# A scan over tokens with eight routed experts: one-bank PSUM tiles for the experts, alternating output banks, and small steps of the scan on GpSimd

## The chip, the core and the metric

One core of a Trainium2 chip runs the whole kernel. The metric is device time in microseconds, from the first instruction to the last. Three runs of the kernel before give a median of 426.35 us (425.26 to 426.58).

Names: PE is TensorE (PEld its weight loads), DVE VectorE, ACT ScalarE, POOL or GpSimd the fourth compute engine, SP the engine that issues most loads. PSUM, in which PE puts its products, has eight banks of 2 KB for each of 128 partitions; the other engines copy or add out of it into SBUF.

## What is computed

A state-space scan over 4 batches x 8 heads x 768 tokens (head size 32, state size 16), then a router that sends each of the 3072 tokens to one of eight experts, by cosine against the experts' embeddings:

```python
for c in range(nc):                      # chunks along the sequence
    cum = cumsum(log_a of the chunk); L = exp(cum_i - cum_j), i >= j
    M = (C @ B^T) * L
    y = M @ x + (C @ state) * exp(cum)
    state = exp(sum(log_a)) * state + sum_j B_j x_j * exp(cum_last - cum_j)
x = y as (3072, 256)
logits = (x/|x|) @ (emb/|emb|).T / tau
e = argmax(logits); gate = probs[e]
out[token] = gate * (relu(x @ w1[e]) @ w2[e])      # 256 -> 1024 -> 256
```

## The kernel before, in words

**Start and scan** (begin(), 1153; scan(), 1188). The sequence is cut into 6 chunks of 128 tokens; a step handles one chunk of two of the four batches, so there are 12 steps. For each step load() (272) brings c, b and x on SP's queue two chunks ahead; scale_c() (285) and scale_x() (306) multiply them by decays and their inverses, on GpSimd except in chunk 0; split_c() (297) masks into two halves on ACT. On PE, inner() (320, L328) multiplies C by B into pg, causal() (335, L338) masks that on DVE, outputs() (344, L354 with the state, L365 within the chunk) goes into py, sums() (372, L379) makes the new part of the state in py, and states() (386) with pass_on() (413) adds it to the old state and scales it, on DVE: reads of PSUM at L399 to L404 and the scaled state at L416. keep_outputs() (422) copies to SBUF on ACT, finish() (430, L434) turns the result to token order and appends the logits in pz, keep_tokens() (440) copies it and keep_rows() (448) writes a chunk's rows to DRAM on SP's queue.

The decays of all heads are computed by decays() (155, last operation L169) for chunks 0 to 3 at the start and for 4 and 5 after step 1. keep_decays() (182, L186) permutes them on PE, writes them to DRAM (fd), and spread_decays() (192) reads them back, repeated over state rows, into F with four DMAs a chunk. For chunk 0, spread_first() (202) does it on PE. scale_emb() (246, L252 to L255) and turn_emb() (258) prepare the router's embeddings; route_consts() (99) makes constants on GpSimd.

Routing goes chunk by chunk behind the scan: pick() (455, last operation L467) makes one-hots of the best expert, count() (472) adds them up, ranks() (479, L487) counts on PE how many tokens of the same expert come before, hots() (492) makes of that a place in a table of 104-row tiles, tables() (527, L530) and add_table() (535) put token numbers there.

**Experts** (moe(), 1317). early() (1309) starts a first job J0 with the first 208 tokens of expert 0 from chunks 0 to 3, while the scan ends; a second job J1 holds further tokens of expert 0, then come seven jobs of up to 416 tokens. gather() (683, L687) fetches a job's tokens by four indirect loads on GpSimd, squares() (694) and gates1() to gates3() make the gate, turn() and keep_turned() (730, 737) transpose the input. J0 uses plain products (plain_up(), 871; plain_down(), 882, L887). All the others use a scheme of seven block products in place of eight: up() (760, L763) for each of two groups g and p = 1 to 7, down() (819, L823) for p = 1 to 7. A product goes into one of three banks of a set (760: `BANK = {1: 0, 6: 0, 7: 0, 4: 0, 2: 1, 5: 2, 3: 2}`), further products are added there, and keep() (771, L775, ACT), c11() to c22() (783 to 797, DVE L785, L789, L793) or o11() to o22() (828 to 842, L831, L835) read the bank between them. turn_out() (846, L850) transposes an output of 104 tokens into the fourth bank, send() (854) scales it by the gate on ACT (L857) and writes it with an indirect DMA on GpSimd (L860). weight_sums() (646) makes the sums of weight blocks that the scheme needs.

**Order.** Everything runs under a manual schedule: each engine works in the order of the code. work_on() (894) writes out one round: the up blocks of job J mixed with the outputs of the job before and the transposes of the next, then the down blocks, mixed with the weights' sums and the first two up blocks of the next job (begin_job(), 961). leftover() (966) counts at the end whether tokens are left that fit in no job, and branches (L998).

**PSUM.** Lines 1376 to 1381 allot the eight banks as three tiles, and take the experts' banks as slices of them:

```python
k.pg = ps.tile([128, 4, 512], F32, name="pg")
k.py = ps.tile([128, 2, 512], F32, name="py")
k.pz = ps.tile([128, 2, 512], F32, name="pz")
k.sets = [[k.pg[:, i] for i in range(3)], [k.py[:, 0], k.py[:, 1], k.pz[:, 0]]]
k.tb = [k.pg[:, 3], k.pz[:, 1]]
```

Of the kernel before, what the change touches and what calls it, by code (L numbers as in the profile page):

```python
# [17 lines left out]
Q = 128  # L18
# [37 lines left out]
def first_consts(k):  # L56
    nc = k.nc
    k.heads = tile_(k, "heads", [128, Q], pool=k.sc)
# [4 lines left out]
    for q in range(4):  # L63
# [15 lines left out]
    s = k.swap[:].rearrange("k (r q t) -> k r q t", q=4, t=2)  # L79
    nc.gpsimd.affine_select(  # L80
        out=s, in_=s, pattern=[[-8, 16], [-1, 4], [-4, 2]], compare_op=ALU.not_equal, fill=1.0, base=0,
        channel_multiplier=1,
    )
# [15 lines left out]
def route_consts(k):  # L99
# [4 lines left out]
    k.rank = tile_(k, "rank", [128, E])  # L104
    nc.gpsimd.tensor_scalar(
        out=k.rank[:], in0=k.step[:, 0:E], scalar1=-1.0, scalar2=float(E), op0=ALU.mult, op1=ALU.add
    )
# [74 lines left out]
def keep_decays(k, kk, ps):  # L182

    nc = k.nc
    n = 128 if kk == 0 else 64
    nc.tensor.matmul(ps, lhsT=k.swap[:], rhs=k.f[:, kk, :], start=True, stop=True)  # L186
    v = k.sc.tile([128, FW], F32, name=f"fs{kk}")
    nc.scalar.copy(out=v[:], in_=ps)
    nc.sync.dma_start(k.fd[4 * kk : 4 * kk + n // 32].rearrange("c b q t s -> (c b q t) s"), v[0:n])


def spread_decays(k, c):
    t = k.ld[c]
    t.f = k.inp.tile([128, NB, FW], F32, name="F", tag="F")
    for b in range(NB):
        k.nc.sync.dma_start(
            t.f[:, b, :],
            k.fd[c, b].rearrange("q t s -> (q t) s").unsqueeze(1).to_broadcast([8, N, FW]),
        )


def spread_first(k):

    nc = k.nc
    for b in range(NB):
        nc.tensor.matmul(
            k.pz[:, b // 2, FW * (b % 2) : FW * (b % 2) + FW], lhsT=k.spread[:, b, :], rhs=k.f[0:32, 0, :],
            start=(b % 2 == 0), stop=True, skip_group_check=True,
        )
    k.fcol = k.sc.tile([128, NB, 2, 2], F32, name="fcol")  # L210
    for i in range(2):
        f = k.pz[:, i, 0 : 2 * FW].rearrange("p (b s) -> p b s", b=2)
        nc.scalar.copy(out=k.fcol[:, 2 * i : 2 * i + 2, 0, :], in_=f[:, :, HQ - 1 : Q : HQ])
        nc.scalar.copy(out=k.fcol[:, 2 * i : 2 * i + 2, 1, :], in_=f[:, :, Q:FW])
# [82 lines left out]
def split_c(k, p):
    s = k.un[p]
    s.cm = k.work.tile([128, 2, 2, 2, HQ], F32, name="cm", tag="cm", bufs=3)
    for v in range(2):  # L300
        k.nc.scalar.activation(  # L301
            s.cm[:, :, :, v, :], s.cp[:].rearrange("p i (h s) -> p i h s", h=2), ACT.Copy, scale=k.tmask[:, v : v + 1]
        )


def scale_x(k, p):
# [5 lines left out]
    eng = k.nc.vector if p == 0 else k.nc.gpsimd  # L312
    eng.tensor_tensor(  # L313
# [72 lines left out]
def states(k, p):  # L386
    nc = k.nc
    tt = nc.vector.tensor_tensor
# [3 lines left out]
    for h in range(2):  # L392
        i = 2 * c + h
        if i == 2 * NC - 1:
            break
        u = k.work.tile([128, 2, D], F32, name="u", tag="u", bufs=6)
        v0, v1 = ps[:, h, :, 0, :], ps[:, h, :, 1, :]
        if i == 0:
            nc.vector.tensor_scalar(out=u[:], in0=v0, scalar1=k.tmask[:, 0:1], scalar2=None, op0=ALU.mult)  # L399
        else:  # L400
            nc.vector.scalar_tensor_tensor(  # L401
                out=u[:], in0=v0, scalar=k.tmask[:, 0:1], in1=k.T[i][:, bb, :], op0=ALU.mult, op1=ALU.add
            )
# [44 lines left out]
def keep_rows(k, c):  # L448
    k.nc.sync.dma_start(k.rows.rearrange("(c b p) w -> c p b w", b=NB, c=NC)[c], k.yt[c][:])
# [5 lines left out]
def pick(k, c):  # L455
    nc = k.nc
    w = k.work
    l = k.yt[c][:, :, LG : LG + E]
    m = w.tile([128, NB], F32, name="m", tag="m")
    nc.vector.reduce_max(out=m[:], in_=l, axis=AX.X)  # L460
    oh = w.tile([128, NB, E], F32, name="oh", tag="oh")
    nc.vector.tensor_tensor(out=oh[:], in0=l, in1=m[:].unsqueeze(2).to_broadcast([128, NB, E]), op=ALU.is_equal)
    nc.vector.tensor_tensor(
        out=oh[:], in0=oh[:], in1=k.rank[:].unsqueeze(1).to_broadcast([128, NB, E]), op=ALU.mult
    )
    nc.vector.reduce_max(out=m[:], in_=oh[:], axis=AX.X)
    nc.vector.tensor_tensor(  # L467
        out=k.ob[:, c], in0=oh[:], in1=m[:].unsqueeze(2).to_broadcast([128, NB, E]), op=ALU.is_equal
# [3 lines left out]
def count(k, c):  # L472
    nc = k.nc
    s = k.work.tile([128, E], F32, name="csum", tag="csum")
    nc.vector.reduce_sum(out=s[:], in_=k.ob[:, c].rearrange("p u e -> p e u"), axis=AX.X)
    nc.vector.tensor_tensor(out=k.sums[:, c + 1, :], in0=s[:], in1=k.sums[:, c, :], op=ALU.add)
# [15 lines left out]
def hots(k, c, at):  # L492
# [401 lines left out]
def work_on(k, J, P, N, parity, last):  # L894
# [71 lines left out]
def leftover(k):  # L966
# [30 lines left out]
    n = nc.values_load(all_i[0:1, 0:1], min_val=0, max_val=LEFT)  # L997
# [155 lines left out]
def begin(k):  # L1153
    k.f = tile_(k, "f", [128, 2, FW], pool=k.sc)
# [3 lines left out]
    k.T, k.ld, k.un, k.yt, k.hot, k.wt = {}, {}, {}, {}, {}, {}  # L1158
    k.later = []
# [280 lines left out]
```

## Time and profile before

| what | value |
| --- | --- |
| median of three runs | 426.35 us |
| the profiled execution, its own time | 418.69 us |
| its span, first to last instruction | 416.9 us |
| busy PE, DVE, ACT, POOL | 288.6, 195.8, 121.1, 105.2 us |
| mean granted clock of TensorE | 0.882 of full speed |
| instructions | 8017 |
| moved by DMA | 36.63 MB |

The profile is of one execution, and the rows below are of that one; its own time stands beside the median of the runs. Busy time is summed over the span, PE's from modelled ends. A wait is put down to what came last before the waiting instruction started; "issue" is time for which the profile shows no cause.

### The profile page before, as it was taken

The numbers are of one execution on the slowest core, as the hardware profiler recorded it, in microseconds if no ns is written. First come the engines' busy times: TensorE is split into PE (matmuls) and PEld (weight loads), VectorE is DVE, ScalarE is ACT, GpSimd is POOL, SyncE is SP. The second block draws the span as 40 slices with busy tenths as digits, with TensorE's granted clock in tenths as the row PEclk, the third lists the DMA queues.
The fourth block names the chain that finished last, engine by engine and source line by source line (L and its number), as shares of the span: only waits on it lengthen the run. The fifth ranks groups of instructions, "written<-read, shape, count | busy, mean of one in ns | idle before, by whom it ended". The sixth has DMA issues, their size and how long they took to land.

```text
span 416.9 us, 8017 instructions
## 1 busy us (share of the span) xinstructions
PE 288.6 (69%) x3168; PEld 240.9 (58%) x3168; DVE 195.8 (47%) x577; ACT 121.1 (29%) x322; POOL 105.2 (25%) x166
## 2 busy tenths in 40 slices
PE   2247785876878688786868776868877676975570
PEld 2125674665656578575748565747766565753450
DVE  3574576364446437175248238236425534726210
ACT  2112321131222223343334234143233333333210
POOL 3621321200201424205133142230522512122003
PEclk9999869588879757999999989996988999999695
DMA  6715439201215813404313313131340100000001
GB/s 177 238 34 155 134 111 347 81 4 55 77 52 171 285 31 124 131 11 142 100 45 123 116 47 105 39 127 20 137 121 18 40 15 26 2 20 14 5 0 34
DMA packets 23448, 36.63 MB, mean 88 GB/s; under 512 B 2457, under 2 KB 16674, under 8 KB 23408
## 3 DMA queue, kind: packets, MB, share of 16 engines
q1 hardware_dynamic: 20160, 29.35, 21.8%
q0 software_dynamic: 3024, 6.67, 5.7%
q8 instruction: 25, 0.41, 0.4%
q14 instruction: 15, 0.12, 0.1%
q10 hardware_dynamic: 224, 0.07, 0.1%
HBM read 29.59 MB, written 6.52 MB: 87 GB/s over the span
## 4 chain that ended last, share of the span: by engine, by line
PE 50%; issue 18%; DVE 11%; ACT 8%; DMA 7%; POOL 2%; POOLq 0%; ACTq 0%; DVEq 0%
PE pg L763 10%; PE pg L823 7%; PE py L763 6%; DMA out_dram<-yof,s_rest 5%; PE py L823 4%; PE pz L763 3%; PE py L354 3%; PE pz L434 3%; PE pz L823 2%; PE py L365 2%; PE pg L328 2%; PE pg L876 2%; ACT yof L857 2%; PE pg L887 1%; DVE h22f L793 1%
## 5 line engine op out<-in xcount | busy, mean ns | idle before, releaser
L860 POOL DMA_INDIRECT out_dram<-yof,s_rest x28 | 28.0, 1001 | 97.6 <-ACT yof L857 94.3
L687 POOL DMA_INDIRECT xgf<-rows,g_rest x28 | 30.9, 1105 | 12.3 <-issue 7.7
L703 POOL TENSOR_TENSOR nrf<-nrf,half 104x4 f32<-104x4 f32 x7 | 7.9, 1122 | 69.6 <-ACT sqf L699 59.0
L425 ACT COPY yT<-py 128x512 f32<-128x512 f32 x12 | 7.0, 586 | 52.1 <-PE py L379 24.0
L763 PE MATMUL pg<-xTf,w 128*128 128x208 f32 (+6 forms) x56 | 13.4, 363 | 8.3 <-ACT cf L775 4.2
L338 DVE TENSOR_TENSOR g<-pg,mask 128x1024 f32<-128x1024 f32 x12 | 14.6, 1219 | 9.3 <-PE pg L328 9.3
L434 PE MATMUL pz<-turn,yT 128*128 128x136 f32 x96 | 18.4, 348 | 0.0
L785 DVE TENSOR_TENSOR h11f<-pg,p1f 128x416 f32<-128x416 f32 (+6 forms) x7 | 3.9, 557 | 30.7 <-PE pg L763 30.7
L313 POOL TENSOR_TENSOR xs<-x,rT 128x512 f32<-128x512 f32 x11 | 11.9, 1085 | 20.1 <-PE py L365 11.8
L354 PE MATMUL py<-cm,T 32*32 32x128 f32 x352 | 16.3, 336 | 0.6 <-DVE u L404 0.6
L365 PE MATMUL py<-g,xs 64*32 64x64 f32 x768 | 13.0, 265 | 5.3 <-issue 5.3
L434 PEld LDWEIGHTS pz<-turn,yT 128*128 128x128 f32 x96 | 15.7, 241 | 1.3 <-issue 0.7
L763 PE MATMUL pg<-xsf,s 128*128 128x208 f32 (+6 forms) x56 | 14.8, 396 | 2.4 <-ACT yof L857 1.7
L763 PE MATMUL py<-xsf,w 128*128 128x208 f32 (+6 forms) x56 | 13.1, 359 | 4.6 <-DVE h22f L793 3.5
L763 PEld LDWEIGHTS pg<-xTf,w 128*128 128x128 f32 x56 | 9.0, 194 | 12.4 <-ACT cf L775 6.2
L294 POOL TENSOR_TENSOR cp<-ct,F 128x256 f32<-128x256 f32 x10 | 6.8, 679 | 36.6 <-DMA F<-fd 20.7
L365 PEld LDWEIGHTS py<-g,xs 64*32 64x32 f32 x768 | 10.1, 126 | 9.3 <-issue 9.3
L763 PE MATMUL pg<-xsf,w 128*128 128x208 f32 (+6 forms) x56 | 13.5, 368 | 2.1 <-ACT xTf L741 1.2
L328 PE MATMUL pg<-cm,bt 32*64 32x128 f32 x384 | 11.6, 367 | 3.9 <-ACT cm L301 3.1
L401 DVE SCALAR_TENSOR_TENSOR u<-py,tmask,T 128x64 f32<-128x64 f32 x20 | 5.7, 283 | 17.7 <-ACT yT L425 17.3
L785 DVE TENSOR_TENSOR h11f<-py,p1f 128x416 f32<-128x416 f32 (+6 forms) x7 | 3.9, 557 | 21.2 <-PE py L763 21.2
L379 PE MATMUL py<-xs,b 64*32 64x64 f32 x384 | 8.3, 269 | 7.9 <-issue 4.8
(356 smaller groups left out, 736.3 us busy)
## 6 DMA issues: line engine op xcount, KB each, us to landing
w<-in_moe_w_dram SPq DMA_DIRECT2D x16, 1024.0 KB
rows<-yt SPq DMA_DIRECT2D x6, 528.0 KB
x<-in_x_dram SPq DMA_DIRECT2D x6, 512.0 KB
ct<-in_CT_dram SPq DMA_DIRECT2D x6, 256.0 KB
bt<-in_BT_dram SPq DMA_DIRECT2D x6, 256.0 KB
b<-in_B_dram SPq DMA_DIRECT2D x6, 256.0 KB
F<-fd SPq DMA_DIRECT2D x20, 65.0 KB
xgf<-rows,g_rest POOLq DMA_INDIRECT x28, 3.1
```

Source lines behind the costliest of these rows:

```text
L313: eng.tensor_tensor(out=s.xs[:].rearrange("p i (h d) -> p (i h) d", d=D), in0=t.x[:, b : b + 2, :].rearrange("p i (h d) -> p (i h) d", d=D ...
L328: nc.tensor.matmul(k.pg[m, q, 128 * i : 128 * i + 128], lhsT=t.bt[r, b + i, m], rhs=s.cm[r, i, h].rearrange("p v s -> p (v s)"), start=Tru ...
L338: k.nc.vector.tensor_tensor(out=s.g[:], in0=k.pg[:, :, 0:256].rearrange("p q (t i) -> p q t i", t=4), in1=k.mask[:].unsqueeze(1).unsqueeze ...
L354: nc.tensor.matmul(k.py[r, h, 128 * i : 128 * i + 128], lhsT=k.T[2 * c + h][r, b + i, :], rhs=s.cm[r, i, h].rearrange("p v s -> p (v s)"), ...
L365: nc.tensor.matmul(k.py[r, h, a : a + HQ], lhsT=s.xs[m, i, n : n + 32], rhs=s.g[m, q, 2 * i + v, :], start=(2 * c + h == 0 and i == 0 and ...
L434: k.nc.tensor.matmul(k.pz[:, i, at : at + Y1], lhsT=yT[:, 2 * i + j].rearrange("p h s -> p (h s)"), rhs=k.turn[:, j, :], start=(j == 0), s ...
L687: k.nc.gpsimd.indirect_dma_start(out=s.x[:, i, 0:W], out_offset=None, in_=k.rows[0:rows, :], in_offset=bass.IndirectOffsetOnAxis(ap=s.g_id ...
L763: s.k.nc.tensor.matmul(bank[:, w * i : w * i + w], lhsT=a[:, 2 * g + i, :], rhs=s.r1[p], start=(p in (1, 2, 5) and i == 0), stop=True, ski ...
L823: s.k.nc.tensor.matmul(bank[:, 0:w], lhsT=a[:, g, :], rhs=r[:, g, 0:w], start=(p in (1, 2, 5) and g == 0), stop=True, skip_group_check=True,)
L857: nc.scalar.activation(y[0:n], bank[0:n, 256 * half : 256 * half + 256], ACT.Copy, scale=s.gate[0:n, i : i + 1])
L860: d = nc.gpsimd.indirect_dma_start(out=k.out[:, :], out_offset=bass.IndirectOffsetOnAxis(ap=s.s_idx[0:n, i : i + 1], axis=0), in_=y[0:n], ...
L876: nc.tensor.matmul(bank[:, 0:n], lhsT=s.wt.w1[:, j, 128 * f : 128 * f + 128], rhs=s.xT[:, j, 0:n], start=(j == 0), stop=(j == KD - 1),)
```

## The change

1. **PSUM.** The scan keeps pg, py and pz. Behind the scan the banks are allotted anew as eight tiles of one bank each: four when pg is free, four when py and pz are. work_on() puts outputs 0 to 3 into the two output banks in alternation (0, 1, 0, 1 in place of 0, 0, 1, 1), with other blocks between.
2. **Scan.** States: DVE only reads PSUM; the sum with the second state and both scalings are GpSimd's, a first masked read is ACT's. GpSimd also makes inside(), across(), count() and half of hots(). pick() has four DVE operations in place of five. The order is new: scale_c() and scale_x() come ahead of outputs(), pick() and count() too, ranks() and tables() behind sums(), beside finish(). The rows and decays are written on ACT's queue. F is read by one DMA for a chunk. The first weights load at step 7, not 5.
3. **Start.** Loads of chunks 1 and 2 are issued earlier, 40 products of zeros run on PE before the first decays, the permutation swap is filled by two selects on GpSimd in place of one, chunk 0's mask and product are one DVE operation, route_consts() and scale_emb() move into step 0, turn_emb() to step 1, the second decays to step 2.
4. **Between.** scan_end() is cut from scan(): J0's gather is issued ahead of its targets, J1's ahead of sort() and of the weights. The count of leftovers moves to job 3, the branch stays.

```diff
 def spread_decays(k, c):
-    for b in range(NB):
-        k.nc.sync.dma_start(t.f[:, b, :], ...)
+    k.nc.sync.dma_start(
+        t.f[:].rearrange("p b s -> p (b s)"),
+        k.fd[c].rearrange("m b s -> m (b s)").unsqueeze(1).to_broadcast([8, N, NB * FW]),
+    )
...
 def inside(k, c):
-    k.nc.vector.tensor_tensor(out=k.whole[:, 2 * c, :], ...)
+    k.nc.gpsimd.tensor_tensor(out=k.whole[:, 2 * c, :], ...)
...
 def states(k, p):
+    u = [k.work.tile([128, 2, D], F32, name="u", tag="u", bufs=6) for h in range(2)]
+    for h in range(1 if last else 2):
+        v0, v1 = ps[:, h, :, 0, :], ps[:, h, :, 1, :]
+        if h == 0 and i > 0:
+            nc.vector.scalar_tensor_tensor(
+                out=u[h][:], in0=v0, scalar=m0, in1=k.T[i][:, bb, :], op0=ALU.mult, op1=ALU.add
+            )
+        else:
+            nc.scalar.activation(u[h][:], v0, ACT.Copy, scale=m0)
+        nc.vector.scalar_tensor_tensor(out=u[h][:], in0=v1, scalar=m1, in1=u[h][:], op0=ALU.mult, op1=ALU.add)
+    pass_on(k, i, bb, u[0])
+    if not last:
+        nc.gpsimd.tensor_tensor(out=u[1][:], in0=u[1][:], in1=k.T[i + 1][:, bb, :], op=ALU.add)
...
 def pass_on(k, i, bb, u):
-    k.nc.vector.tensor_tensor(
+    k.nc.gpsimd.tensor_tensor(
...
 def keep_rows(k, c):
-    k.nc.sync.dma_start(...)
+    k.nc.scalar.dma_start(...)
...
 def count(k, c):
-    nc.vector.reduce_sum(out=s[:], in_=k.ob[:, c].rearrange("p u e -> p e u"), axis=AX.X)
-    nc.vector.tensor_tensor(out=k.sums[:, c + 1, :], in0=s[:], in1=k.sums[:, c, :], op=ALU.add)
+    nc.gpsimd.tensor_tensor(out=s[:], in0=k.ob[:, c, 0:2], in1=k.ob[:, c, 2:4], op=ALU.add)
+    nc.gpsimd.tensor_tensor(out=s[:, 0], in0=s[:, 0], in1=s[:, 1], op=ALU.add)
+    nc.gpsimd.tensor_tensor(out=k.sums[:, c + 1, :], in0=s[:, 0], in1=k.sums[:, c, :], op=ALU.add)
...
 def work_on(k, J, P, N, parity, last):
-            P.turn_out(i, TB[i // 2], i % 2)
+            P.turn_out(i, TB[i % 2], i // 2)
...
     J.up(0, 3, X); J.keep("c", X[2])
+    out(0)
     J.up(0, 2, X); J.c11(0, X)
-    out(0); out(1)
+    out(1)
...
     J.up(1, 5, Y); J.keep("p5", Y[2]); q5 = J.p5
+    out(2)
...
-    out(2); out(3)
+    out(3)
...
 def begin(k):
     load(k, 0)
+    load(k, 1)
+    expert_emb(k)
+    load_late_decays(k)
+    first_consts(k)
+    for i in range(40):
+        nc.tensor.matmul(k.pg[:, 3, 0:128], lhsT=k.zero[:], rhs=k.zero[:], start=True, stop=True)
+    decays(k, 0)
...
 def scan(k):
         if s > 0:
             inner(k, s)
             causal(k, s)
             if s + 1 < NP:
                 split_c(k, s + 1)
+        if s + 2 < NP:
+            scale_c(k, s + 2)
+            scale_x(k, s + 2)
         if s >= 5 and s % 2:
-            hots(k, (s - 5) // 2, at((s - 5) // 2))
+            hots(k, (s - 5) // 2, at)
+        if s >= 4 and s % 2 == 0:
+            pick(k, (s - 4) // 2)
+            count(k, (s - 4) // 2)
         if s > 0:
             outputs(k, s - 1)
...
+        if s >= 4 and s % 2 == 0:
+            ranks(k, (s - 4) // 2, at)
         if s >= 2:
             finish(k, s - 2)
...
+            k.banks = four("right", "bx")
+            scan_end(k)
+        late = four("left", "by")
+        k.sets = [k.banks[0:3], late[0:3]]
+        k.tb = [k.banks[3], late[3]]
```

where four() allots four PSUM tiles of 128 x 512 from a pool whose reuse waits tile by tile.

## Rows read from the trace of the kernel before

**Rows 1.** The page: busy time of an engine, share of the span, instructions.

```profile
PE 288.6 (69%) x3168; PEld 240.9 (58%) x3168; DVE 195.8 (47%) x577; ACT 121.1 (29%) x322; POOL 105.2 (25%) x166
```

**Rows 2.** Windows by stage: length, busy us (instructions) by engine, clock, DMA share, GB/s.

```profile
24.00:108.00 84.00, 59.13 (x1830) 48.18 (x1814) 45.83 (x154) 20.54 (x43) 13.79 (x16) 0.82 0.35 111
108.00:141.40 33.40, 23.85 (x216) 19.15 (x214) 17.27 (x87) 7.42 (x23) 5.62 (x6) 0.90 0.48 157
141.40:160.00 18.60, 15.96 (x68) 14.31 (x69) 6.67 (x18) 5.40 (x15) 5.53 (x8) 0.50 0.22 63
160.00:389.50 229.50, 169.42 (x886) 143.54 (x885) 111.28 (x275) 78.17 (x212) 62.62 (x83) 0.94 0.22 69
389.50:404.50 15.00, 12.07 (x56) 10.03 (x56) 2.38 (x11) 3.01 (x13) 1.04 (x1) 0.85 0.01 3
```

**Rows 3.** Waits of PE, 12 to 108 us: total us, times, longest.

```profile
PE pg L487 <- DVE ob L467: 7.7, 4, 2.4
...
PE py L365 <- issue: 5.3, 3, 2.5
PE py L379 <- issue: 4.8, 2, 3.7
PE pz L186 <- DVE f L169: 4.6, 1, 4.6
```

**Rows 4.** Waits of PE, 160 to 405 us.

```profile
PE pz L850 <- ACT yof L857: 8.0, 6, 1.4
...
PE pg L850 <- ACT yof L857: 5.9, 6, 1.5
PE pg L823 <- DVEq L998: 5.3, 1, 5.3
```

**Rows 5.** Timeline of PE in the expert rounds: start, us, work, idle time before it.

```profile
209.68 0.96 PE L763 MATMUL pg<-xTf,w 128*128 128x204 f32 x4 [0.64 <-ACT p5f L775]
...
267.90 0.81 PE L763 MATMUL pz<-xsf,s 128*128 128x192 f32 x4
268.55 0.81 PE L763 MATMUL py<-xTf,w 128*128 128x192 f32 x4
...
293.21 1.46 PE L823 MATMUL pz<-h22f,s 128*128 128x192 f32 x8
294.51 1.46 PE L823 MATMUL py<-t2f,s 128*128 128x192 f32 x8
```

**Rows 6.** Timeline of PE, behind a group of gaps in the next round.

```profile
309.26 1.43 PE L763 MATMUL pz<-xsf,s 128*128 128x184 f32 x4
```

**Rows 7.** Timeline of PE: start of step 2, first and last block of J0's ups, downs.

```profile
32.54 1.16 PE L328 MATMUL pg<-cm,bt 32*64 32x128 f32 x32
...
117.03 1.75 PE L876 MATMUL pg<-xTh,w 128*128 128x208 f32 x4 [0.81 <-ACT xTh L741]
...
130.97 3.08 PE L887 MATMUL pg<-hTh,w 128*128 128x208 f32 x16 [0.43 <-ACT hTh L880]
```

**Rows 8.** The page, costliest groups: gathers (count, busy, mean ns, idle before).

```profile
L687 POOL DMA_INDIRECT xgf<-rows,g_rest x28 | 30.9, 1105 | 12.3 <-issue 7.7
```

**Rows 9.** Timeline of DVE and GpSimd, 17 to 24 us.

```profile
18.56 3.58 DVE L253 TENSOR_TENSOR emb_r<-emb_r,tau 8x1 f32<-8x1 f32 x1
...
20.45 0.67 POOL L294 TENSOR_TENSOR cp<-ct,F 128x256 f32<-128x256 f32 x1
21.09 1.04 POOL L313 TENSOR_TENSOR xs<-x,rT 128x512 f32<-128x512 f32 x1
```

**Rows 10.** Timeline of PE within a step of the scan.

```profile
63.82 1.19 PE L434 MATMUL pz<-turn,yT 128*128 128x136 f32 x8
...
68.22 1.08 PE L354 MATMUL py<-cm,T 32*32 32x128 f32 x32
69.23 0.86 PE L365 MATMUL py<-g,xs 64*32 64x64 f32 x64
```

**Rows 11.** Source line L313, the product x: ns least, median, most.

```profile
L313 DVE TENSOR_TENSOR xs<-x,rT x1: 693/693/693, 12.9 to 12.9; 128x512 f32<-128x512 f32 x1
```

More of the change, by code (lines that the diff above doesn't have):

```diff
@@ L78, in first_consts @@
     nc.gpsimd.memset(k.swap[:], 0.0)
[L79 to L83, printed above, removed]
+    s = k.swap[:].rearrange("k (c q t b) -> k c q t b", c=4, q=4, t=2)
+    for t in range(2):
+        nc.gpsimd.affine_select(
+            out=s[:, :, :, t, :], in_=s[:, :, :, t, :], pattern=[[-32, 4], [-1, 4], [-8, NB]],
+            compare_op=ALU.not_equal, fill=1.0, base=-4 * t, channel_multiplier=1,
+        )
     k.ident = tile_(k, "ident", [128, 128])
@@ L103, in route_consts @@
     k.step = ramp(k, "step", [128, LEFT], [[1, LEFT]])
[L104 to L107, printed above, removed]
+    k.same = tile_(k, "same", [128, NB * E])
+    nc.gpsimd.memset(k.same[:], 1.0)
+    nc.gpsimd.memset(k.same[:, 0 : NB * E : E], 0.0)
     k.at104 = ramp(k, "at104", [128, NT + 1], [[TR, NT + 1]])
@@ L206, in spread_first, with keep_first @@
         nc.tensor.matmul(
-            k.pz[:, b // 2, FW * (b % 2) : FW * (b % 2) + FW], lhsT=k.spread[:, b, :], rhs=k.f[0:32, 0, :],
+            k.pz[:, b // 2, Q * (b % 2) : Q * (b % 2) + Q], lhsT=k.spread[:, b, :], rhs=k.f[0:32, 0, 0:Q],
             start=(b % 2 == 0), stop=True, skip_group_check=True,
         )
[L210 to L214, printed above, removed]
+    for b in range(NB):
+        nc.tensor.matmul(
+            k.pz[:, b // 2, 256 + 2 * (b % 2) : 258 + 2 * (b % 2)], lhsT=k.spread[:, b, :], rhs=k.f[0:32, 0, Q:FW],
+            start=False, stop=True, skip_group_check=True,
+        )
+def keep_first(k):
+    nc = k.nc
+    k.fcol = k.sc.tile([128, 2, NB, 2], F32, name="fcol")
+    nc.scalar.copy(
+        out=k.fcol[:, 0].rearrange("p (i b) h -> p i (b h)", i=2),
+        in_=k.pz[:, :, HQ - 1 : 2 * Q : HQ],
+    )
+    nc.scalar.copy(out=k.fcol[:, 1].rearrange("p (i b) h -> p i (b h)", i=2), in_=k.pz[:, :, 256:260])
 def cols(k, c):
     if c == 0:
-        return k.fcol[:, :, 0, :], k.fcol[:, :, 1, :]
+        return k.fcol[:, 0], k.fcol[:, 1]
     f = k.ld[c].f
@@ L1157, in begin @@
     k.whole = tile_(k, "whole", [128, 2 * NC, NB], pool=k.sc)
-    k.T, k.ld, k.un, k.yt, k.hot, k.wt = {}, {}, {}, {}, {}, {}
-    k.later = []
+    k.T, k.ld, k.un, k.yt, k.hot, k.wt, k.later = {}, {}, {}, {}, {}, {}, []
     k.nil = tile_(k, "nil", [1, 1])
@@ L1303, in scan @@
     k.J1.gather()
+    sort(k, n)
+    load_weights(k, 1)
+    for f in range(4, KF):
+        J.plain_up(f, X[f % 3])
     k.J1.s_idx = targets(k, "late", late[:], g)
-    load_weights(k, 1)
+    k.J0.s_idx = targets(k, "early", k.early[:], k.J0.g_idx)
     load_weights(k, 2)
 def early(k):
-    v = k.table[:, 0, 0:2]
-    g = indices(k, "early", v)
-    t = targets(k, "early", v, g)
-    k.J0 = Job(k, k.ep, "h", [TR, TR], g, t, k.wt[0])
+    k.early = tile_(k, "early", [TR, 2])
+    k.nc.vector.tensor_copy(out=k.early[:], in_=k.table[:, 0, 0:2])
+    k.J0 = Job(k, k.ep, "h", [TR, TR], indices(k, "early", k.early[:]), None, k.wt[0])
     k.J0.gather(EARLY * NB * Q)
+    return k.J0
 def moe(k):
@@ L1373 @@
     k.list = tc.dram_tile([E * T, 1], I32, name="list")
[L1374 removed]
+    k.fd = tc.dram_tile([NC, NH, NB, FW], F32, name="fd")
     enter = ctx.enter_context
[L1376 to L1381 removed]
     k.const = enter(tc.tile_pool(name="const", bufs=1))
@@ L1385, with four @@
     k.ep = enter(tc.tile_pool(name="ep", bufs=1))
+    def four(side, name):
+        p = enter(tc.tile_pool(name=name, bufs=1, space=PSUM, side=side, reuse_waits="tile"))
+        return [p.tile([128, 512], F32, name=f"{name}{i}") for i in range(4)]
     with tc.manual_schedule():
```

270 lines of the change are left out of this document (129 added, 141 removed).

## The prediction, made before the change was run

> **What bounds the kernel now.** I read the page's busy shares first: no engine is full; TensorE (PE) leads with 288.6 of 416.9 us [rows 1]. Then the windows by stage [rows 2]. In the scan (24 to 108, after the start) PE is busy 59.1 of 84. From 108 to 141.4 the early job J0 runs, to 160 the first part of J1, and 160 to 389.5 holds seven rounds, each from the down blocks of one job to those of the next: 229.5 us, 32.8 a round, PE busy 169.4, idle 60.1. Every other engine is under half there, so the stage hangs on PE and on what PE waits for. Third, PE's waits. In the scan it waits 7.7 us for one-hots (L487), 4.6 for the second decays (L186), and 10.1 for nothing that the profile shows, inside L365 and L379 [rows 3]. In the expert stage it waits for copies by ACT and sums by DVE out of PSUM, in groups of 1 to 8 us; two that lead stand at the top of [rows 4].
>
> Fourth, what those waits are. The block at 209.68 writes bank 0 of pg and starts after the ACT copy of p5, which reads bank 2 of pg: another bank of the same tile. Blocks that alternate between pz and py run without a wait, 0.65 us from start to start for an up block of 192 columns (267.90 to 268.55 [rows 5]) and 1.30 for a down block (293.21 to 294.51). So the waits go by tile, not by bank, and the time is lost twice: as idle time, and as the drain that a wait exposes (the waiting block shows as 0.96, its neighbour comes 0.65 later).
>
> **Expert rounds: one-bank tiles, outputs in alternating banks.** A round is 14 up blocks, 7 down blocks, 2 groups of input transposes (about 0.45 each) and 4 of outputs (about 0.3; both estimated from the 0.16 of one instruction, 0.65 / 4). Dense, at the mean width of 192, that is 14 x 0.65 + 7 x 1.30 + 0.9 + 1.2 = 20.3 us. Waits on one and the same bank stay, estimated from the queues: up 7 of the second half after DVE's sum (0.4), up 4 after DVE, which has three other operations before its sum (0.9), down 3 after p5's copy, which stands behind four squares on ACT (0.6): 1.9. Outputs now wait 13.9 us in 12 places [rows 4], 2.0 a round, since two use one tile; with 0 and 1 in different tiles and other blocks before 2 and 3 I take none. 22.2 x 7 = 155. I add 2 for the branch at L998: most of its 5.3 us [rows 4] is the count of leftovers ahead of it, 12 DVE operations, which move into job 3 beside PE work. And 7 for stretches in which a block takes 1.43 [rows 6] against 0.81 [rows 5]: they follow gaps that go, and I keep about half. 229.5 becomes 164: **-65.5**. DVE (111 us) and ACT (78) fit into 164 [rows 2], GpSimd's 63 too, so no new bound comes.
>
> **J0 and J1.** J0's 8 up blocks last from 117.03 to 130.97 [rows 7], as each waits for the ReLU of the one before, in another bank. Dense (208 columns, 0.70) they are 5.6, with tables, ranks and counts between them 7.6: -6.3. The downs lose one wait: -1. The gather is issued right after the table, ahead of the five target operations, and J0's transposes no longer stand around the last finish(): -2.5. Together **-9.8**. J1's gather moves ahead of sort() and of 4 MB of weights; J0's downs cover its landing. J1 up to its downs takes 18.6 us at granted clock 0.50 [rows 2]; the same waits go, but the next job's gather (four indirect loads of 1.1 us one after another on GpSimd [rows 8], then their landing, some 3 by estimate) caps it near 13: **-5.6**. The last downs, 15.0 [rows 2], become 7 x 1.2 + 1.4: **-5.2**. The tail after 404.5 (four scatters one after another on GpSimd) stays.
>
> **Start.** PE is idle most of it, so 40 warm-up matmuls cost nothing: they need only a memset and end before the first decays, whose load and eight DVE operations PE awaits; the extra select for swap ends before its matmul as well. Loads of chunks 1 and 2 go earlier; on SP the second F and the load between stand behind the write of fd, which nothing needs sooner. What decides is the embedding chain: DVE's L253, an 8x1 product, lasted 3.58 us [rows 9] ahead of step 1. It comes back a step later, ahead of step 2, behind GpSimd's 16 routing constants and its pow. So step 2 starts at about 28.6 instead of 32.54 [rows 7]: -4. That the first products x and the masks change engines is covered by this chain, and the 4.6 for the decays are within it.
>
> **Scan.** Then ten steps to the end at 108.2: 7.57 us each, 6.5 without the 10.1 us that show no cause. The 7.7 for one-hots go, as ranks() now stands behind sums(). DVE gives up to GpSimd three state operations of 64 columns a step (and one to ACT), the counts, wholes, places and Z. A product of 256 columns takes GpSimd 0.67, of 512 1.04 [rows 9]: 0.30 + 1.45 ns a column, so 0.39 for 64 and 0.3 for the smallest. It then has 0.67 + 1.04 + 3 x 0.39 a step, and in two steps 3 counts, 2 wholes and 2 places at 0.3 and a Z at 0.5: 4.2 a step. It is hidden beside PE, barely: PE's dense step is 1.0 for L354 (from its start to the next), 0.9 for L365, 1.2 for L434 [rows 10], about 0.6 each for L328 and L379 at the same pace, and the tables of every other step, less some overlap: 4.4; if the cover goes, the first rival has the price. Waits are added: GpSimd's count waits for DVE's one-hot, and behind it stand the state products, for which the next outputs() wait. I take 5.1 a step: PE's 4.4, and 0.7 for reading the states out of PSUM between sums() and the next outputs(). Eight writes (rows, decays) go from SP to ACT, about 0.4 us of issue each, on an engine busy 20.5 of 84 [rows 2]. One DMA for F instead of four frees SP's issue, for which nothing waits: 0. Weights at step 7 instead of 5 leave the last F free. Of the 10.1 us, which fall while big transfers run (their cause the trace does not show), I keep 7.5, bounds 0 and 20. 28.6 + 51 + 7.5 = 87 against 108.2: **-21** with the start, bounds -32 (no such stalls, cheaper GpSimd operations) and 0.
>
> Here a page speaks against the change. The row: xs of 512 columns takes 1.04 us on GpSimd and 0.69 on DVE [rows 9, 11], 1.5 times. The Trainium skill, "GPSIMD Engine Reference", section 3, states 1.96 times for a two-input product; by it, as an estimate, the moved operations would grow to some 5.0 a step in all and the scan by 2.5 us. The row decides.
>
> **Sum.** 418.7 (the profiled execution's own time) - 65.5 - 9.8 - 5.6 - 5.2 - 21 = 311.6. The median, 426.35, is 7.7 above that execution; carried over by share or in full: **318 us**.
>
> **Rivals.** *The scan gains little.* L253 began at 18.56 and ended with GpSimd's back-to-back run of products, at 22.13 [rows 9]: a DVE operation with two SBUF inputs waits as long as GpSimd keeps working. With GpSimd near full, picks and places wait, state sums stand behind them on DVE, and GpSimd's state products behind those. If its small operations cost twice my estimate, a step takes 6.4 and the scan ends near 100; at 108, if the unexplained stalls grow too. For it: the row, and 4.2 of 5.1. Against: the causal product, with one input in PSUM, keeps its time beside GpSimd. 318 + 13 to 21: 335. By the Trainium skill, "SBUF — State Buffer", section "Who interferes with whom", both engines share a port that one instruction holds whole; the trace agrees, with 3.58 us.
>
> *The waits are not by tile.* Then only the order of outputs and gathers helps, 26 us of the 86 of the expert terms: 378. Against: py and pz alternate freely.
>
> *Slower: the clock.* If TensorE, once dense, were granted its lower level (1.2 instead of 2.4 GHz) in the rounds, seven would take 2 x 142 + 2 = 286, 122 over my term: 440. It decides from about eight tenths of the stage. Against: 0.94 granted at 74% busy, 0.50 in J1 with its narrow blocks and gaps [rows 2].
>
> **How the numbers follow.** Forecast 0.70; little gain in the scan 0.18; waits not by tile 0.07; clock 0.03; other losses 0.02. The range is 300 to 348: below, the scan's bound and 6 us of lower clock less; above, the second case and 13 us of expert waits that I called gone. A difference of 0.3% (1.3 us) is about what a measurement of this kernel tells from none: faster 0.95, same 0.01, slower 0.04.
>
> **What would show it.** Rounds near 23 us; PE's idle time in the expert stage down from 60 to about 15; J0's up blocks within 8; the scan over at 87, with GpSimd busy 40 to 55 us in it instead of 14. It is wrong if blocks to different banks still wait for p5's copy, if the granted clock falls in dense rounds, or if DVE's picks last over a microsecond in most steps.

## The result, and the profile after

The changed kernel takes 299.46 us (median of four runs, 297.36 to 300.09), the one before 425.81 beside it: ratio 0.708, 95% interval 0.698 to 0.718. The forecast was 318, range 300 to 348: faster as forecast, by 126 us in place of 108, and half a us under the low end. The profiled execution took 300.09 us, span 298.3. Its windows, cut at the same events as [rows 2] (columns as there; the first line is the start, the last the tail):

```profile
0.00:24.00 24.00, 13.30 (x299) 10.60 (x299) 8.38 (x29) 5.09 (x14) 13.29 (x51) 0.66 0.75 235
24.00:90.00 66.00, 50.82 (x1690) 41.59 (x1690) 35.58 (x94) 22.19 (x50) 30.91 (x81) 0.87 0.41 126
90.00:113.00 23.00, 18.84 (x213) 17.50 (x212) 15.47 (x75) 7.17 (x22) 9.30 (x18) 1.00 0.54 183
113.00:123.20 10.20, 9.71 (x69) 9.27 (x69) 6.28 (x18) 4.87 (x15) 5.83 (x8) 0.83 0.66 219
123.20:274.90 151.70, 141.77 (x886) 135.04 (x885) 109.17 (x274) 74.93 (x211) 67.22 (x83) 1.00 0.34 105
274.90:287.30 12.40, 11.33 (x64) 10.10 (x64) 3.11 (x13) 4.48 (x17) 1.50 (x2) 0.91 0.01 3
287.30:298.30 11.00, 0.04 (x1) 0.00 (x0) 0.00 (x0) 0.57 (x2) 3.84 (x8) 0.66 0.11 32
```

The seven rounds (fifth line) are dense: PE is busy 141.8 of 151.7, at full granted clock. By stage, the change in the profiled executions against the forecast's terms:

| stage | before, us | after, us | change | forecast |
| --- | --- | --- | --- | --- |
| start and scan, to the last outputs() | 108.2 | 90.0 | -18.2 | -21 |
| to J1's first up block | 33.2 | 23.0 | -10.2 | -9.8 |
| J1's up blocks | 18.6 | 10.2 | -8.4 | -5.6 |
| seven rounds | 229.5 | 151.7 | -77.8 | -65.5 |
| last down blocks (274.9 to 285.1 after) | 15.0 | 10.2 | -4.8 | -5.2 |
| tail | 12.4 | 13.2 | +0.8 | 0 |
| sum | | | -118.6 | -107.1 |

PE's timeline, where an output stands between up blocks (154.97 to 155.88), and J0's up and down blocks (97.01 to 103.61 and after). An up block is four instructions, and blocks that follow each other stand in one row. L783, L843, L870, L896 and L907 are the L763, L823, L850, L876 and L887 of before:

```profile
154.97 0.38 PE L870 MATMUL bx<-ident,yTf 128*104 128x128 f32 x2
155.18 0.86 PE L783 MATMUL by<-xTf,w 128*128 128x204 f32 x4
155.88 0.38 PE L870 MATMUL by<-ident,yTf 128*104 128x128 f32 x2
...
97.01 2.36 PE L896 MATMUL bx<-xTh,w 128*128 128x208 f32 x12
...
103.61 5.79 PE L907 MATMUL bx<-hTh,w 128*128 128x208 f32 x32
```

Nothing waits in these rows. J0's eight up blocks last 6.6 us against 13.9 [rows 7], and start about 0.73 apart.

### The profile page after: what moved, and what is told of

Read it like the earlier page. It is cut to its first block, busy times and chain, and to the rows that moved or that the text cites. A ratio compares the mean times of both kernels' runs of the same rounds, so it can differ in the third digit from the quotient of the medians.

```text
span 298.3 us, 8109 instructions
## 1 busy us (share of the span) xinstructions
PE 245.8 (82%) x3216; PEld 224.1 (75%) x3216; DVE 178.0 (60%) x499; ACT 119.3 (40%) x328; POOL 131.9 (44%) x248
## 4 chain that ended last, share of the span: by engine, by line
PE 50%; issue 17%; DVE 12%; DMA 8%; POOL 5%; ACT 4%; SPq 1%; POOLq 1%; ACTq 0%; DVEq 0%
PE by L783 9%; PE bx L783 8%; PE bx L843 6%; PE by L843 5%; PE pz L449 4%; PE py L369 3%; DMA out_dram<-yof,s_rest 3%; DMA F<-fd 3%; POOL out_dram L880 3%; PE pg L343 2%; PE py L380 2%; PE bx L896 2%; PE bx L907 2%; ACT sqf L719 2%; DVE g L353 1%
## 5 line engine op out<-in xcount | busy, mean ns | idle before, releaser
L880 POOL DMA_INDIRECT out_dram<-yof,s_rest x28 | 32.8, 1172 | 40.4 <-ACT yof L877 37.4
L783 PE MATMUL by<-xsf,w 128*128 128x208 f32 (+6 forms) x56 | 12.5, 348 | 5.2 <-DVE h22f L813 3.5
L814 ACT ACTIVATE h22f<-h22f 128x416 f32<-128x416 f32 (+6 forms) x14 | 7.3, 523 | 19.5 <-DVE h22f L813 19.5
L328 POOL TENSOR_TENSOR xs<-x,rT 128x512 f32<-128x512 f32 x12 | 12.5, 1047 | 5.7 <-ACT fcol L226 5.7
L394 PE MATMUL py<-xs,b 64*32 64x64 f32 x384 | 7.7, 256 | 8.7 <-issue 5.1
L783 PE MATMUL bx<-xsf,w 128*128 128x208 f32 (+6 forms) x56 | 12.0, 337 | 3.1 <-DVE h22f L813 2.2
L783 PEld LDWEIGHTS by<-xsf,w 128*128 128x128 f32 x56 | 9.2, 192 | 6.7 <-DVE h22f L813 4.2
L431 POOL TENSOR_TENSOR T<-u,whole 128x64 f32<-128x64 f32 x22 | 6.4, 294 | 15.5 <-DVE u L418 14.7
L369 PEld LDWEIGHTS py<-cm,T 32*32 32x32 f32 x352 | 10.0, 116 | 3.9 <-issue 2.2
L394 PEld LDWEIGHTS py<-xs,b 64*32 64x32 f32 x384 | 5.3, 121 | 9.7 <-issue 5.6
L380 PE MATMUL py<-g,xs 64*32 64x64 f32 x768 | 11.7, 238 | 0.8 <-issue 0.8
L719 ACT ACTIVATE sqf<-xgf 104x256 f32<-104x256 f32 x28 | 11.6, 415 | 1.6 <-ACTq L1026 1.0
L380 PEld LDWEIGHTS py<-g,xs 64*32 64x32 f32 x768 | 9.2, 112 | 4.0 <-issue 3.9
L783 PEld LDWEIGHTS bx<-xsf,w 128*128 128x128 f32 x56 | 9.2, 189 | 3.9 <-DVE h22f L813 2.6
L343 PE MATMUL pg<-cm,bt 32*64 32x128 f32 x384 | 11.5, 343 | 0.7 <-DVE cm L314 0.3
```

Of the source, the lines that this page charges most:

```text
L328: k.nc.gpsimd.tensor_tensor(out=s.xs[:].rearrange("p i (h d) -> p (i h) d", d=D), in0=t.x[:, b : b + 2, :].rearrange("p i (h d) -> p (i h) ...
L343: nc.tensor.matmul(k.pg[m, q, 128 * i : 128 * i + 128], lhsT=t.bt[r, b + i, m], rhs=s.cm[r, i, h].rearrange("p v s -> p (v s)"), start=Tru ...
L369: nc.tensor.matmul(k.py[r, h, 128 * i : 128 * i + 128], lhsT=k.T[2 * c + h][r, b + i, :], rhs=s.cm[r, i, h].rearrange("p v s -> p (v s)"), ...
L380: nc.tensor.matmul(k.py[r, h, a : a + HQ], lhsT=s.xs[m, i, n : n + 32], rhs=s.g[m, q, 2 * i + v, :], start=(2 * c + h == 0 and i == 0 and ...
L394: k.nc.tensor.matmul(k.py[r, h, 256 + 64 * i : 320 + 64 * i], lhsT=t.b[m, b + i, r], rhs=s.xs[m, i, :].rearrange("p (t q d) -> p q t d", t ...
L719: nc.scalar.activation(sq[:], s.x[:, i, :].rearrange("p (j w) -> p j w", j=KD)[:, :, 0:128], ACT.Square, accum_out=s.nr[:, i : i + 1],)
```

## The experiments

Four runs undo or isolate one part; each was timed three times beside the kernel before. No run isolates the earlier gathers of J0 and J1 or the earlier loads of the start.

**Banks as slices of larger tiles.**

```diff
-        return [p.tile([128, 512], F32, name=f"{name}{i}") for i in range(4)]
+        if name == "bx":
+            t = p.tile([128, 4, 512], F32, name=name)
+            return [t[:, i] for i in range(4)]
+        t = [p.tile([128, 2, 512], F32, name=f"{name}{i}") for i in range(2)]
+        return [t[0][:, 0], t[0][:, 1], t[1][:, 0], t[1][:, 1]]
```

> The changed kernel (299.5 us), with the experts' eight banks taken as slices of larger tiles again, one of four banks and two of two; the order of work, the alternating outputs and the scan stay. Theory (waits go by tile): blocks again wait for copies out of other banks; the seven rounds go from 151.7 us to between 185 and 215, J0's eight up blocks from 6.6 to about 13, the time to 340 to 375. First rival (the order of the outputs made the gain): the rounds stay within 8 us of 151.7 and the time is 300 to 308. Second rival (the gaps cost the clock more than themselves): as the theory, and the granted clock of the rounds falls below 0.96 from 1.00.

Measured 391.63 us (ratio 0.912, 0.904 to 0.920); the profiled execution took 394.26. A row of PE's waits, then the windows of J0's up blocks, of the rounds and of the last down blocks:

```profile
PE bx L843 <- ACT p5f L795: 6.9, 4, 2.2
```

```profile
99.90:121.80 21.90, 15.84 (x48) 11.01 (x46) 8.45 (x37) 2.75 (x8) 3.06 (x5) 0.50 0.25 84
...
146.10:358.80 212.70, 164.13 (x885) 137.80 (x885) 111.63 (x275) 77.06 (x213) 62.59 (x83) 0.97 0.24 75
358.80:380.00 21.20, 18.25 (x58) 15.26 (x59) 2.38 (x11) 2.77 (x11) 1.04 (x1) 0.54 0.00 1
```

The rounds take 212.7 us, within the theory's range; the down block waits for p5's copy again, 6.9 us in four places. Work was the same, so the tiles put 61 us back into the rounds; the 2.6 us by which this execution lies above the median are small beside that. The total went past the theory's 375: J0's up blocks take 21.9 us in place of 6.6, over the theory's 13, and the last down blocks 21.0 in place of 10.2. The clock of the rounds is 0.97, above the 0.96 that the second rival needed. But in the two short stretches the second rival's mechanism has a part: the granted clock is 0.50 and 0.54 there, and nearly all their blocks last 1.75 and 2.7 us in place of about 0.95 and 1.36.

**Tiles alone.** The kernel before with eight one-bank tiles behind the scan (the scan's three tiles move into a pool that ends with it):

```diff
+        ps = enter(tc.tile_pool(name="px", bufs=1, space=PSUM, reuse_waits="tile"))
+        bank = [ps.tile([128, 512], F32, name=f"px{i}") for i in range(8)]
+        k.sets = [bank[0:3], bank[4:7]]
+        k.tb = [bank[3], bank[7]]
```

> The kernel before with only one part of the change: behind the scan the experts' banks are eight one-bank tiles. Outputs, scan, start and the gathers are those of before. Theory (waits go by tile): rounds 229.5 to about 168, J1's ups 18.6 to 14, the last down blocks 15 to 12; 350 to 362 in all against 426. Rival (tiles matter only together with the order): less than 25 us gained, over 400.

Measured 361.46 us (ratio 0.850, 0.844 to 0.857): 64 us gained by the tiles without any change of order, 53 of them in the rounds (176.6 in place of 229.5; the theory had 168). Its rounds, and J0's up blocks, which still use the scan's tiles as in the kernel before:

```profile
159.60:336.20 176.60, 144.05 (x886) 134.69 (x884) 110.21 (x275) 77.23 (x212) 61.92 (x83) 0.99 0.29 90
```

```profile
118.00:137.00 19.00, 16.00 (x56) 12.42 (x57) 11.11 (x50) 2.82 (x9) 1.97 (x2) 0.56 0.32 110
```

**Outputs as before.**

```diff
-            P.turn_out(i, TB[i % 2], i // 2)
+            P.turn_out(i, TB[i // 2], i % 2)
...
-    out(0)
     J.up(0, 2, X); J.c11(0, X)
-    out(1)
+    out(0); out(1)
```

(and in the same way send(), out(2), out(3) and the last job)

> The changed kernel with the outputs placed as before: two by two into the same output bank, and issued in pairs; the one-bank tiles stay. Theory: the second of a pair waits for ACT's copy of the first, 1.2 us on the mean of the twelve waits of the profile before; two a round in seven rounds make 14 to 17 us: 312 to 317. Rival (with one-bank tiles the copy is hidden): under 3 us, 299 to 303.

Measured 325.25 us (ratio 0.766, 0.760 to 0.771): 26 slower than the changed kernel. One pair in PE's timeline:

```profile
161.60 0.38 PE L870 MATMUL bx<-ident,yTf 128*104 128x128 f32 x2
163.44 0.43 PE L870 MATMUL bx<-ident,yTf 128*104 128x128 f32 x2 [1.47 <-ACT yof L877]
```

The second output of a pair waits 1.47 us for the copy of the first out of the same bank, one-bank tiles or not. Such waits sum to 18.0 us in 13 places (8.5, 8.0, 1.5): the theory's mechanism, but more than its 14 to 17. The rounds grew by 20.6 (172.3 less 151.7), and J1 by 3.3; the other 2 lie behind the scan, where the program is the same (next run). So the tiles alone bring 64 us, and the order of outputs 24 on top of them.

**The order within a step, as before** (GpSimd keeps its work; scale_c(), scale_x(), tables() and add_table() move likewise):

```diff
-        if s >= 4 and s % 2 == 0:
-            pick(k, (s - 4) // 2)
-            count(k, (s - 4) // 2)
...
+        if s >= 4 and s % 2 == 0:
+            pick(k, (s - 4) // 2)
+            ranks(k, (s - 4) // 2, at)
+            count(k, (s - 4) // 2)
```

> The changed kernel with the order within a step of the scan as before: products c and x behind the token copies, picks, ranks and counts at the end of a step, tables one step earlier. GpSimd keeps its new work. Theory (the order takes the waits for one-hots away): PE again waits 6 to 9 us for them, and the time is 305 to 310. Rival (picks of four operations are early enough in either order): 298 to 302.

Measured 310.91 us (ratio 0.730, 0.724 to 0.735): 11.5 slower, a little past the theory's 310. PE's waits in the scan, then the windows of the scan and of the stretch up to J0's first up block:

```profile
PE pz L506 <- DVE ob L485: 3.9, 3, 1.8
...
PE pz L550 <- POOL T L431: 3.1, 3, 1.2
```

```profile
24.00:93.40 69.40, 52.03 (x1688) 42.62 (x1688) 32.23 (x88) 22.50 (x50) 31.08 (x77) 0.84 0.37 119
93.40:104.30 10.90, 9.06 (x136) 7.80 (x135) 3.71 (x18) 2.35 (x5) 4.49 (x11) 0.69 0.30 96
```

The waits for one-hots are back, at 3.9 us where the kernel before had 7.7 and the theory 6 to 9, and tables wait 3.1. From step 2 to the last outputs() the scan takes 68.9 us in place of 62.6: 6.3 more, near these 7.0. It ends only 3.4 later (93.4 against 90.0), as step 2 starts at 24.5 in place of 27.4. The stretch behind it takes 3.9 more (10.9 against 7.0), at granted clock 0.69 against 1.00. Not all of that is the edit's: the same short stalls of 0.4 us inside L380 that stand in this stretch here stand in the run above and in that with the count at the end, whose programs are the changed kernel's up to there, and they take 9.0 us for it. J0 and J1 take another 3.2. That the later gaps lowered the clock and were paid a second time fits, and was not shown.

The next four were timed five times, on one chip.

**The changed kernel again.**

> The changed kernel itself, timed again beside the runs of this group: 298 to 301 us.

299.09 us (ratio 0.707, 0.703 to 0.711).

**Small operations back on DVE.**

```diff
-    k.nc.gpsimd.tensor_tensor(
+    k.nc.vector.tensor_tensor(
         out=k.T[i + 1][:, bb, :], in0=u[:], ...
```

(and likewise the sum of states(), inside(), across(), count() and hots().)

> The changed kernel with every small operation that it gave to GpSimd back on DVE, in the same places of the order: the state's sum and scalings, wholes, counts, places and the product Z; ACT keeps its masked read. Theory of the change as forecast (DVE was in the way in the scan, GpSimd takes 4.2 us a step beside PE): the scan grows by 3 to 8 us: 302 to 308. Rival (DVE, at 35.6 of 66 us in the scan, has room, and its operations are shorter, 0.22 against 0.29 us for the state's scaling): within 1.5 us or faster, 296 to 301.

302.94 us (0.712, 0.707 to 0.717): 3.9 slower by the medians, at the theory's low end, 2 by the ratios, whose intervals overlap; all six executions, from 300.09, lie above all six of the changed kernel, to 300.08. Groups of lines, first of the changed kernel, then of this one:

```profile
L431 POOL TENSOR_TENSOR T<-u,whole 128x64 f32<-128x64 f32 x22 | 6.4, 294 | 15.5 <-DVE u L418 14.7
L540 POOL TENSOR_TENSOR Z<-ob,o 128x128 f32<-128x128 bf16 x6 | 3.5, 590 | 0.5
```

```profile
L431 DVE TENSOR_TENSOR T<-u,whole 128x64 f32<-128x64 f32 x22 | 4.8, 221 | 0.4
L540 DVE TENSOR_TENSOR Z<-ob,o 128x128 f32<-128x128 bf16 x5 | 1.5, 292 | 0.2
```

Moving work to the engine on which it takes 1.3 to 2 times as long paid, but little: 2 to 4 of the 126 us.

**No products of zeros before the first decays.**

```diff
-    for i in range(40):
-        nc.tensor.matmul(k.pg[:, 3, 0:128], lhsT=k.zero[:], rhs=k.zero[:], start=True, stop=True)
```

> The changed kernel without the 40 products of zeros before the first decays. Forecast's theory (PE is idle there, they cost and bring nothing): 298 to 301 us. First rival (they are what brings the granted clock down: 1.00 until they end and 0.50 to 0.62 from 6 to 30 us, where the kernel before shows 1.00 throughout): the clock stays at 1.00 up to 30 us, and 1 to 3 us go: 296 to 299. Second rival (they help, as a later drop of the clock is avoided): over 301.

298.88 us (0.707, 0.703 to 0.711): no difference. The window from 6 to 30 us, of the changed kernel and then of this one:

```profile
6.00:30.00 24.00, 12.08 (x345) 8.65 (x346) 9.95 (x19) 5.14 (x18) 13.63 (x48) 0.53 0.74 232
```

```profile
6.00:30.00 24.00, 14.30 (x347) 10.64 (x346) 9.95 (x19) 5.04 (x18) 14.00 (x48) 1.00 0.71 230
```

By these windows the first rival looks right about the clock, 0.53 with the products and 1.00 without. PE's timeline says otherwise; three rows of the changed kernel, then two of this run:

```profile
5.55 1.12 PE L208 MATMUL pz<-f,spread 32*128 32x128 f32 x8 [0.66 <-DVE f L172]
...
8.43 1.16 PE L343 MATMUL pg<-cm,bt 32*64 32x128 f32 x32 [0.31 <-DVE cm L314]
...
32.32 0.69 PE L343 MATMUL pg<-cm,bt 32*64 32x128 f32 x32
```

```profile
5.55 2.04 PE L208 MATMUL pz<-f,spread 32*128 32x128 f32 x8 [5.55 <-DVE f L172]
...
10.06 1.16 PE L343 MATMUL pg<-cm,bt 32*64 32x128 f32 x32 [0.24 <-DVE cm L314]
```

The thirty-two products of L343 last 1.16 us in both, under a row of 0.50 and under one of 1.00; they last 0.69 at 32.32, where the granted clock is 1.00. Right behind the forty products of zeros, L208 and L213 last 1.12 and 0.95 us, without them 2.04 and 1.70. So what stands right behind the products of zeros ran quicker, not slower, and the products further on last as long with them as without. The 1.00 of this run is no reading of the clock: its trace has no entry on the clock before 31.8 us. The first rival is wrong about the time too: step 2 waits for the embeddings either way, and starts at 26.9 in place of 28.2 in the run beside it.

**First weights in four loads, a step apart** (512 KB each, on ACT's queue in place of SP's):

```diff
-        if s == 7:
-            load_weights(k, 0, 0)
+        if 7 <= s <= 10:
+            first_weights(k, s - 7)
```

> The changed kernel with the first job's weights (2 MB) in four loads of 512 KB on ACT's queue, issued in steps 7, 8, 9 and 10, in place of two on SP's issued one behind the other at 51 us. Theory (PE's stalls of 5.1 us at L394 and of 1.5 at L449, for which the profile shows no cause, come when a burst of transfers holds the DMA engines above 0.9): the long stall goes and shorter ones may stay: 293 to 297. Rival (the stall has nothing to do with the burst): it stays, at 53 us, and the time is 298 to 301.

296.64 us (0.702, 0.697 to 0.706), the fastest kernel of all; four of its six executions lie under the fastest of the changed kernel's six, though the two ratios' intervals overlap by 0.003. PE's timeline at the stall, of the changed kernel and then of this one:

```profile
53.38 0.39 PE L394 MATMUL py<-xs,b 64*32 64x64 f32 x16
58.88 0.46 PE L394 MATMUL py<-xs,b 64*32 64x64 f32 x14 [5.11 <-issue]
```

```profile
53.02 0.34 PE L394 MATMUL py<-xs,b 64*32 64x64 f32 x14 [1.35 <-issue]
```

The stall stays at the same instruction, the last 14 of L394's products of that step, but lasts 1.35 us. In the changed kernel's two profiles it is 5.11 and 4.14, in three more runs with the same program up to there 5.06, 4.28 and 3.25; with the transfers issued as before it is 1.82. So its place belongs to the program, and its length changes with the transfers: the theory in part. Queue and pace changed together, and no run tells them apart.

The last four were timed three times.

**The count of leftovers at the end again.**

```diff
-        if j == 3:
-            count_leftover(k)
...
 def leftover(k):
+    count_leftover(k)
```

> The changed kernel with the count of leftovers back at the end, ahead of the branch. Theory of the forecast (most of the 5.3 us ahead of the last down blocks were the count's twelve DVE operations; 0.4 is left): 4 to 5.5 us slower, 303 to 305. Rival (the branch itself waits for something else that the new order ended): under 1.5 us, 298 to 301.

308.38 us (307.40 to 312.47). The wait ahead of the last down blocks, among PE's waits:

```profile
PE bx L843 <- ACTq L1027: 4.8, 1, 4.8
```

It takes 4.8 where the changed kernel has 0.4, and the last round 26.6 us against 21.5: the theory's size. The median is 9 above 299.5, past the theory's 305. The profiled execution shows 7.2, of which 1.4 lie ahead of the rounds, where the program is the same. What the other 2 of the median are I leave open.

**F by four DMAs, rows and decays on SP.**

```diff
+    for b in range(NB):
+        k.nc.sync.dma_start(t.f[:, b, :], k.fd[c][:, b, :].unsqueeze(1).to_broadcast([8, N, FW]))
...
-    k.nc.scalar.dma_start(k.rows...)
+    k.nc.sync.dma_start(k.rows...)
```

> The changed kernel with the transfers' issue as before: F by four DMAs a chunk, decays and rows written from SP's queue. Forecast's theory (SP's issue keeps nothing waiting): within 1.5 us, 298 to 301. Rival (on SP a rows write waits for its token copy and holds back the loads behind it, and twenty issues of F in place of five come later): chunk loads land later and PE waits in the scan, 302 to 310.

300.52 us (299.52 to 302.81): within the forecast's 1.5 us. Reading F by one DMA and writing rows and decays from ACT's queue moved nothing that can be told.

**The embeddings earlier.**

```diff
         if s == 0:
-            route_consts(k)
             scale_emb(k)
         if s == 1:
-            turn_emb(k)
+            route_consts(k)
         if s == 2:
+            turn_emb(k)
```

> The changed kernel with the embeddings' scale ahead of GpSimd's routing constants, the constants one step later, and the embeddings' transposes ahead of the first finish() in step 2 (both transposes, then both copies). Theory (the embedding chain holds step 2: PE idle 6.0 and 1.8 us at L277): step 2 starts at 20 to 23 us, not 27.4, and 3 to 6 us go: 293 to 296. Rival (behind it the loads and products of chunk 1 and 2 are due next): step 2 comes earlier, and PE waits for products x or c in steps 2 to 5 instead; 297 to 300.

305.70 us (304.74 to 307.05), 6 slower than the changed kernel. PE's waits, 8 to 100 us, and the window behind the scan:

```profile
PE pg L345 <- issue: 4.5, 2, 4.2
PE pz L451 <- POOL turn L273: 3.8, 1, 3.8
PE py L396 <- issue: 3.6, 1, 3.6
```

```profile
92.90:104.00 11.10, 10.25 (x58) 9.78 (x53) 3.95 (x17) 3.03 (x7) 2.93 (x11) 0.54 0.19 61
```

Step 2 starts at 23.6 and not at 27.4, after a stall of 4.2 us that the wait for the embeddings had covered; then PE waits 3.8 for GpSimd's copies into turn, which my edit put behind the routing constants. At the end of the scan everything won is lost: the last outputs() start at 88.8, against 90.0 and 87.7 in the two profiles of the changed kernel. What follows takes 11.3 us in place of 7.0, with three short stalls of 0.4 us and a clock of 0.54; 2 of these 4.3 come with the same stalls in runs without this edit (9.0 us, above). Both expectations fall. What sets the stall of 4.2 and the short ones is open.

**All three edits together.**

> The changed kernel with three edits together: no products of zeros, first weights paced over four steps on ACT's queue, embeddings as in the run on them alone. If the gains add, 2.5 from the weights and 3 to 6 from the embeddings, and the full clock in the start helps once nothing holds step 2: 289 to 294. If the transfers of the first chunks hold the start: 295 to 298.

300.69 us (298.94 to 307.59): the gains do not add.

## Why the forecast held, and where its terms were off

**Waits go by tile.** Shown from both sides (61 us in the rounds put back by slices, 64 in all gained by tiles alone). The rival that they do not is out: 378 was its time.

**The rounds: 164 forecast, 151.7 measured.** The dense part, 20.3 x 7 = 142, was right: PE is busy 141.8. The other terms were too high. PE's waits from 123 to 287 us:

```profile
PE by L783 <- DVE h22f L813: 3.5, 4, 1.1
PE bx L783 <- DVE h22f L813: 2.2, 3, 0.9
PE by L783 <- DVE h12f L809: 1.7, 4, 0.7
PE bx L783 <- DVE h12f L809: 0.9, 3, 0.4
PE by L843 <- ACT p5f L795: 0.6, 2, 0.4
...
PE bx L843 <- PEq L1026: 0.4, 1, 0.4
...
PE bx L843 <- ACT p5f L795: 0.3, 1, 0.3
```

Up 4 waits 0.8 a round (forecast 0.9), up 7 0.4 (0.4); down 3 waits 0.9 us in all in three rounds, where the forecast had 0.6 in each, 4.2. The branch costs 0.4, not 2. The 7 us kept for low clock are 0: the granted clock is 1.00. Together these terms (same-bank waits, branch, low clock) were 22 and measured 9.9.

**The clock.** The rival on the other side (440 us) asked for 1.2 GHz in dense rounds. The level granted is the upper one, 2.4 GHz, all through them, and 0.97 with the gaps of the slices, 0.94 before: denser work went with a higher clock.

**J0 and J1.** J0 as forecast (6.6 against 7.6 for its ups). J1's cap of 13, by the landing of the next job's gather, was an estimate in part without a row, and did not bind: 10.2.

**Start and scan: -21 forecast, -18.2 measured.** Step 2 starts at 27.4 (28.6), so the start was right, by the mechanism forecast (below). The ten steps take 62.6, 7.7 of it without a shown cause (7.5 forecast), so 5.5 a step in place of 5.1. GpSimd was sized too dear: 0.29 for 64 columns and 0.20 for the smallest in place of 0.39 and 0.3, busy 30.9 us where the text named 40 to 55. So the rival of a full GpSimd had a row for its mechanism, but not its condition: GpSimd was busy 30.9 of 66 us, and the price did not come. The timeline of DVE and GpSimd in the changed kernel:

```profile
22.98 1.46 DVE L265 TENSOR_TENSOR emb_r<-emb_r,tau 8x1 f32<-8x1 f32 x1
...
23.39 1.04 POOL L328 TENSOR_TENSOR xs<-x,rT 128x512 f32<-128x512 f32 x1
```

The 8x1 product ends at 24.44, with GpSimd's product (24.43), as in [rows 9]. The Trainium skill, "SBUF — State Buffer", section "Who interferes with whom", says that the two engines share a port that one instruction locks; by these rows the trace agrees.

**The median.** Of the 7.7 us by which the median of before lay above its profiled execution, the forecast carried over 6.4 (318 less 311.6). The changed kernel's profiled execution lies 0.6 above its median, so this step alone is 7.0 of the 18.5 us by which the forecast was high. The rounds are 12.3, J1 2.8 and J0 0.4; the scan (-2.8), the last down blocks and the tail go the other way.

## What to carry to other kernels

Where a block waits for a copy out of a bank that it does not write, look at how the banks are allotted: one tile for each bank took 64 us here, before any order was touched. Then alternate banks for results that are read at once (24 us). A wait taken away in a stretch where others are due next can bring nothing or cost time, as the embeddings did.

## What the runs showed of the hardware that was not expected

**Stalls that stand multiples of 256 records apart.** The longest of PE's stalls without a cause in the profile lasts 5.11 us in the changed kernel, at a DMA share of 0.97, and 1.35 with the weights paced. Counted in the order of start, 2241 of PE's records (weight loads, products and waits) stand ahead of it in both. The run without the products of zeros, in which PE has 80 records fewer ahead, stalls behind 2241 records too, and so at another line:

```profile
60.05 1.14 PE L343 MATMUL pg<-cm,bt 32*64 32x128 f32 x28 [2.70 <-issue]
```

The changed kernel's stalls at 74.33, 77.78, 81.71 and 85.58 us (1.52, 0.56, 0.25 and 0.26) stand behind 3009, 3265, 3521 and 3777, each a multiple of 256 further; with the 5.11 they are all of the scan's 7.7 us without a cause. The five that make up the 10.1 us of [rows 3] in the kernel before stand so too, behind 961, 1473, 2497, 2753 and 3521. The DMA queues of the changed kernel from 53 to 59.5 us (packets, MB, share of 16 engines):

```profile
q1 hardware_dynamic: 677, 1.50, 76.0%
q10 hardware_dynamic: 336, 0.35, 15.3%
q8 instruction: 1, 0.02, 1.0%
q14 instruction: 1, 0.01, 0.3%
```

The Trainium skill, "Runtime: NRT & Kernel Launch", section "Instruction fetch mechanics", says that an engine's instructions come in by DMA in blocks of 256 and that this is mostly hidden. By the counts the trace agrees on the 256; a stall of 5.11 us is not hidden. Two packets of such queues fall into the stall, among 1.9 MB of data. That of q8 (16 KB) starts 2.8 us into the stall and ends 1.3 us before PE goes on; in the run without the products of zeros its like ends 1.3 us before, and with the weights paced, where it starts 1.0 us ahead of the stall, 1.4. That PE waited for this packet, and the packet for the data, is what the counts and times suggest; no run changed the packets alone.

**A granted clock of 1.00 at the start says nothing.** Without the products of zeros the row reads 1.00 from 6 to 30 us, and the products there last as long as under 0.50 (1.16 us for L343, above). The trace of the kernel before has no entry on the clock ahead of 35.5 us either, and its L328 lasts 1.16 us at 32.54 [rows 7]. The time of a known product is the safer reading there.

**The same blocks at two levels.** The same eight up blocks of J0 took 13.9 us before, at a granted clock of 0.86, and 18.7 in the run with the tiles alone, where the granted clock over them was 0.56.
